# Taking the inverse sequence DFT of a spectral filter from radix 4 to radix 8, beside a gated MLP on the same core

## The chip, the cores and the metric

The kernel runs on one core of a Trainium2 chip. The metric is the device time of one execution in microseconds (us). The kernel before takes 262.6 us (median of 16 runs, 262.2 to 263.7). The record marks each execution as fast or slow by its time and its clock; every run that is quoted here is marked fast.

Engines are named as in the profile: PE (TensorE matmuls), PEld (its weight loads), DVE (VectorE), ACT (ScalarE), POOL (GpSimd), SP (the queue that issues most DMAs). "Start to start" is the distance between the starts of neighbouring instructions in the timeline. It is shorter than the duration of one record, because records of one engine overlap. PSUM is the memory in which the kernel keeps PE's results (tiles such as pd, gps, ups, dn, cs, ut, fp), SBUF the one for all other tiles. Line numbers such as L397 differ between kernels; the names of tiles do not.

## The reference, cut to what matters

```
xn = layernorm(x)                                  # x: 1 x 2048 x 512, bf16
A  = irfft2( rfft2(xn) * (w_r + 1j*w_i) )          # over sequence and features
B  = ( gelu(xn @ w_gate) * (xn @ w_up) ) @ w_down  # 512 -> 1792 -> 512
out = x + A + B
```

All the DFTs are done as matmuls with constant tables of cosines and sines. Along the sequence (2048) the DFT is split: the index is k = 2048/R·m + k0 and the position is s = R·t + r. A butterfly of radix R over m runs on DVE; a matmul over k0 runs on PE.

## The kernel before

Four groups of work matter.

- **MLP**: gps and ups (gate and up projection), then hT, then dn (down projection). It has 4 chunks of 14 column blocks. Per block PE runs 8 matmuls of 512 columns, ACT makes sq, gsb and sg, DVE makes wtl, z, m and hT. Each row block adds dn to x on DVE, into bsp.
- **Forward DFT**: pd (along features), then cs (along the sequence), then a radix-4 butterfly on DVE and the product with w_r + i·w_i (tiles qq, bf, XFk, tm).
- **Inverse along the sequence**: a radix-4 butterfly on DVE into YY, then the matmuls of ut with the table Rt, which ACT copies to UT.
- **Inverse along features**: fp, added to bsp on DVE, and out.

The instruction order of each engine is fixed when the kernel is built. Code marked `hp()` is placed as early as its inputs allow; everything else goes in program order, with the MLP ahead of the DFT's work on DVE.

The part that is changed, cut:

```python
for kc in range(4):                       # k = 512 m + 4 i + kc
    Fkc, WRk, WIk = ...                   # loaded by SP
    for r in range(4):
        cbsb = p3q.tile([P, 2, 256], BF16, tag="cbsb", bufs=2)
        ...  # cs: 2 x 4 matmuls of 512 columns, ACT copies to qq and cbsb, DVE adds
    ...  # radix-4 butterfly forward: 16 additions; product with w: 24
    ...  # radix-4 butterfly inverse: 16 additions into bi and YY, 4 negations, 8 tiny copies

UT = p3ut.tile([P, 4, 4, D], BF16)
Rt = p3r.tile([P, 4, 2, 4, D], BF16)      # 4 MB
nc.gpsimd.dma_start(out=Rt[:], in_=rview)
with hp():
  for rp in range(4):
    for t in range(4):
        ut = p3u.tile([P, D], FP32)
        for kc in range(4):
            for pi_, (lt, rh) in enumerate(pairs):   # two pairs: (YY part, Rt part)
                nc.tensor.matmul(ut[:], lhsT=lt, rhs=rh, ...)   # 512 columns
        nc.scalar.copy(out=UT[:, rp, t, :], in_=ut[:])
```

## Time and profile before

| | before |
|---|---|
| time, median | 262.6 us |
| span of the profiled run | 260.3 us |
| PE / DVE / ACT busy | 240.8 / 183.3 / 140.9 us |
| ut on PE | 187.5 to 215.4 us |
| last write to YY on DVE | 178.1 us |

The first part of the page of the kernel before, busy time, and its PE and DVE rows of 40 equal slices (each digit is the busy share in tenths):

```profile
PE 240.8 (92%) x1120; PEld 107.3 (41%) x1120; DVE 183.3 (70%) x613; ACT 140.9 (54%) x286; POOL 11.6 (4%) x20
PE   0398999999999999999999999999999999989993
DVE  3996844448996899997999999995820005872573
```

PE has work in nearly every slice after the first. DVE is nearly full from slice 10 to slice 27 (counted from 1) and idle in slices 31 to 33, under ut.

The table of stretches of the kernel before (stretch, its length, busy us and instructions of PE, PEld, DVE, ACT and POOL, granted clock, DMA share, GB/s):

```profile
10.00:60.00 50.00, 48.54 (x253) 23.48 (x254) 30.95 (x86) 40.54 (x83) 3.08 (x4) 1.00 0.52 170
60.00:180.00 120.00, 117.64 (x529) 50.81 (x528) 112.79 (x440) 69.60 (x150) 0.57 (x1) 1.00 0.19 64
180.00:248.00 68.00, 66.73 (x307) 29.79 (x306) 27.00 (x60) 28.85 (x52) 0.00 (x0) 1.00 0.10 43
```

From 60 to 180 us PE is idle for 2.4 us and DVE for 7.2 us.

The timeline of PE in the kernel before, around ut (start, length, engine, line, instruction, count):

```profile
186.87 0.81 PE L209 MATMUL ups<-xnT,wu 128*128 128x512 bf16 x3
187.51 28.04 PE L397 MATMUL ut<-Rt,YY 128*128 128x512 bf16 x128
215.39 0.38 PE L209 MATMUL ups<-xnT,wu 128*128 128x512 bf16 x1
```

ut is one unbroken block. From 187.51 to the next start at 215.39 are 27.88 us, 218 ns for each of 128 matmuls. The MLP is not finished then; it goes on afterwards.

The last instruction that writes YY, from the view of that tile (duration ns min/median/max, first and last start):

```profile
L365 DVE COPY YY<-YY x16: 143/152/156, 77.4 to 178.1; 128x1 bf16<-128x1 bf16 x16
```

PE's waits in the kernel before, the longest (who waited for whom, us in total, times, longest):

```profile
PE tp L189 <- DVE xn L183: 10.2, 2, 10.0
PE dn L234 <- DVE hT L229: 1.2, 2, 0.9
PE cs L295 <- ACT cbsb L291: 1.2, 3, 0.5
```

Ten of PE's 19.5 idle us are the start, before the first input has arrived and is normalised.

### The profile page before, as it was taken

Reading aid. Unit: us, or ns where it says so; the run is one execution under the profiler, and the core shown is the slowest. Engines: PE = TensorE matmul, PEld = TensorE weight load, DVE = VectorE, ACT = ScalarE, POOL = GpSimd, SP = SyncE. Lnnn points to the kernel's source line nnn. Section 1 sums busy time; section 2 is a strip of 40 time slices with the busy share of each in tenths; the row PEclk is TensorE's granted clock in tenths of the full one; section 3 lists DMA queues with packets and bytes.
Section 4 is the critical chain, followed back from the end, with each engine's and each line's share of the span. In section 5 each row is a group of like instructions: output and inputs, shape, how many; then the busy total and the mean of one; then the engine's idle time right before and its main releaser. Section 6 shows DMA issues by size and latency. Waiting matters only on the chain.

```text
span 260.3 us, 3447 instructions
## 1 busy us (share of the span) xinstructions
PE 240.8 (92%) x1120; PEld 107.3 (41%) x1120; DVE 183.3 (70%) x613; ACT 140.9 (54%) x286; POOL 11.6 (4%) x20
## 2 busy tenths in 40 slices
PE   0398999999999999999999999999999999989993
PEld 0354444444444444444444444344444444434441
DVE  3996844448996899997999999995820005872573
ACT  1489987768433587974155799422843336920000
POOL 8530000000000000000000000000000000000000
PEclk9999999999999999999999999999999999999999
DMA  7999930004041503000500000038500000000134
GB/s 251 356 337 371 323 99 1 0 3 161 0 109 36 181 0 81 4 1 20 181 21 23 0 0 0 20 95 382 233 3 0 0 0 1 3 1 0 43 120 161
DMA packets 10242, 23.56 MB, mean 91 GB/s; under 512 B 816, under 2 KB 7088, under 8 KB 9584
## 3 DMA queue, kind: packets, MB, share of 16 engines
q1 hardware_dynamic: 8400, 13.12, 15.2%
q0 software_dynamic: 1824, 10.22, 10.8%
q8 instruction: 9, 0.15, 0.2%
q14 instruction: 9, 0.07, 0.1%
HBM read 21.24 MB, written 2.10 MB: 90 GB/s over the span
## 4 chain that ended last, share of the span: by engine, by line
PE 45%; DVE 37%; ACT 11%; issue 4%; DMA 1%; DVEq 0%; ACTq 0%
PE ut L397 9%; DVE hT L229 7%; PE gps L203 7%; PE ups L209 7%; PE dn L234 6%; DVE z L224 5%; PE fp L415 5%; DVE m L228 4%; PE cs L295 4%; PE pd L264 3%; ACT sg L226 3%; PE cs L286 3%; ACT sq L215 2%; DVE bsp L241 2%; DVE stats L174 2%
## 5 line engine op out<-in xcount | busy, mean ns | idle before, releaser
L203 PE MATMUL gps<-xnT,wg 128*128 128x512 bf16 x224 | 60.9, 381 | 0.1
L209 PE MATMUL ups<-xnT,wu 128*128 128x512 bf16 x224 | 59.6, 379 | 0.1
L229 DVE TENSOR_TENSOR hT<-m,ups 128x512 bf16<-128x512 bf16 x56 | 38.3, 683 | 27.4 <-PE ups L209 25.2
L234 PE MATMUL dn<-wd,hT 128*128 128x512 bf16 x224 | 53.7, 379 | 1.7 <-DVE hT L229 1.2
L215 ACT ACTIVATE sq<-gps 128x512 bf16<-128x512 f32 x56 | 33.2, 593 | 20.6 <-PE gps L203 20.0
L226 ACT ACTIVATE sg<-z 128x512 bf16<-128x512 bf16 x56 | 35.3, 631 | 15.1 <-DVE z L224 13.4
L234 PEld LDWEIGHTS <-hT 128*128 128x128 bf16 x224 | 21.8, 97 | 30.9 <-DVE hT L229 3.7
L209 PEld LDWEIGHTS <-wu 128*128 128x128 bf16 x224 | 21.8, 98 | 27.1 <-issue 2.0
L217 ACT CAST gsb<-gps 128x512 bf16<-128x512 f32 x56 | 32.6, 582 | 0.0
L203 PEld LDWEIGHTS <-wg 128*128 128x128 bf16 x224 | 21.9, 98 | 25.2 <-issue 0.7
L228 DVE TENSOR_TENSOR m<-sg,gsb 128x512 bf16<-128x512 bf16 x56 | 23.6, 421 | 10.6 <-ACT sg L226 10.5
L397 PE MATMUL ut<-Rt,YY 128*128 128x512 bf16 x128 | 27.9, 379 | 0.1
L224 DVE TENSOR_TENSOR z<-wtl,gsb 128x512 bf16<-128x512 bf16 x56 | 23.6, 421 | 3.6 <-ACT gsb L217 2.8
L219 DVE TENSOR_SCALAR wtl<-sq 128x512 bf16<-128x512 bf16 x56 | 16.1, 288 | 8.1 <-ACT sq L215 8.1
L397 PEld LDWEIGHTS <-YY 128*128 128x128 bf16 x128 | 12.5, 98 | 15.3 <-issue 0.4
L286 PE MATMUL cs<-Pt,Fkc 128*128 128x512 bf16 x64 | 18.4, 379 | 0.2 <-ACT cbsb L300 0.2
L402 ACT CAST UT<-ut 128x512 bf16<-128x512 f32 x16 | 9.3, 584 | 16.2 <-PE ut L397 16.2
L241 DVE TENSOR_TENSOR bsp<-xblk,dn 128x512 bf16<-128x512 bf16 x16 | 10.9, 683 | 9.8 <-PE dn L234 9.8
L295 PE MATMUL cs<-Pt,Fkc 128*128 128x512 bf16 x64 | 16.4, 378 | 1.3 <-ACT cbsb L291 1.2
L189 PE MATMUL tp<-ident,xn 128*128 128x128 bf16 x64 | 7.1, 254 | 11.2 <-DVE xn L183 10.2
L264 PE MATMUL pd<-Gt,xnT 128*128 128x512 bf16 x64 | 16.4, 379 | 0.0
L415 PE MATMUL fp<-Ginv,UT 128*128 128x512 bf16 x64 | 15.2, 378 | 0.3 <-DVE osb L419 0.3
(65 smaller groups left out, 200.0 us busy)
## 6 DMA issues: line engine op xcount, KB each, us to landing
Fkc<-cF SPq DMA_DIRECT2D x4, 1024.0 KB, 4.9
Rt<-cR POOLq DMA_DIRECT2D x1, 4096.0 KB, 12.7
xt<-in_A_x_dram SPq DMA_DIRECT2D x4, 512.0 KB, 5.8
xblk<-in_A_x_dram SPq DMA_DIRECT2D x16, 128.0 KB, 3.0
out_dram<-osb SPq DMA_DIRECT2D x4, 512.0 KB, 2.6
wd<-in_B_w_down_dram POOLq DMA_DIRECT2D x2, 896.0 KB, 16.2
wg<-in_B_w_gate_dram POOLq DMA_DIRECT2D x4, 384.0 KB, 16.0
wu<-in_B_w_up_dram POOLq DMA_DIRECT2D x4, 384.0 KB, 16.0
```

The lines of the kernel that those rows point to most:

```text
L203: nc.tensor.matmul(gps[:], lhsT=wg[:, dt, fc * P:(fc + 1) * P], rhs=xnT[:, dt, 4 * c:4 * c + 4, :], start=(dt == 0), stop=(dt == 3),)
L209: nc.tensor.matmul(ups[:], lhsT=wu[:, dt, fc * P:(fc + 1) * P], rhs=xnT[:, dt, 4 * c:4 * c + 4, :], start=(dt == 0), stop=(dt == 3),)
L215: nc.scalar.activation(out=sq[:], in_=gps[:], func=ACT.Square)
L217: nc.scalar.copy(out=gsb[:], in_=gps[:])
L224: tt(out=z[:], in0=wtl[:], in1=gsb[:], op=ALU.mult)
L226: nc.scalar.activation(out=sg[:], in_=z[:], func=ACT.Sigmoid, scale=2.0)
L228: tt(out=m1[:], in0=sg[:], in1=gsb[:], op=ALU.mult)
L229: tt(out=hT[:, fc, :], in0=m1[:], in1=ups[:], op=ALU.mult)
L234: nc.tensor.matmul(dn[:], lhsT=hT[:, fc, r * P:(r + 1) * P], rhs=wd[:, fc, :], start=(fc == 0), stop=(fc == 13),)
L295: nc.tensor.matmul(cs2[:], lhsT=Fkc[:, 1, b, :], rhs=Pt[:, b, :], start=(T == 0), stop=(T == 3),)
L397: nc.tensor.matmul(ut[:], lhsT=lt, rhs=rh, start=(kc == 0 and pi_ == 0), stop=(kc == 3 and pi_ == 1),)
L415: nc.tensor.matmul(fp[:], lhsT=UT[:, r, t, c * P:(c + 1) * P], rhs=Ginv[:, t, :], start=(t == 0), stop=(t == 3),)
```

## The change

The butterfly after the product takes 8 values instead of 4. What remains for the matmul is a sum over 256 instead of 512 frequencies, so each of the 8 values of r has an output only 256 columns wide. The number of ut matmuls stays at 128 (8 r, 4 tiles, 2 halves q, 2 parts); their width halves. The table Rt halves to 2 MB. On DVE, two radix-8 butterflies replace four radix-4 ones: 52 additions and 4 scalings each, against 16 additions each. To fit in memory, cbsb, WRk, WIk and tm lose their second buffers; XFk gets a second one, because two blocks now feed one butterfly. x is viewed as rows 8·tau + rho, so the forward tables and the loads of x are permuted too. The forward DFT stays at radix 4.

The core of the diff:

```diff
-        for kc in range(4):
+        for kc in (0, 2, 1, 3):
...
-                cbsb = p3q.tile([P, 2, 256], BF16, tag="cbsb", bufs=2)
+                cbsb = p3q.tile([P, 2, 256], BF16, tag="cbsb", bufs=1)
...
-            tt(out=bi[:, 0, 0, 0:257], in0=z0r, in1=z2r, op=ALU.add)
-            ... (16 additions, 4 negations, 8 tiny copies for each kc)
+            if kc >= 2:
+                q = kc - 2
+                ... ins: 8 values, even ones from XF_by_kc[q], odd ones from XF_by_kc[kc]
+                dft8(ins, outs_, SC)        # 52 additions, 4 scalings
+                ... (8 negations, 16 tiny copies)
...
-        Rt = p3r.tile([P, 4, 2, 4, D], BF16)
+    Rt = p3r.tile([P, 2, 2, 8, 256], BF16)
...
-        for rp in range(4):
+            for rp in range(8):
                 for t in range(4):
-                ut = p3u.tile([P, D], FP32)
-                for kc in range(4):
+                    if t % 2 == 0:
+                        ut2 = p3u.tile([P, 2, 256], FP32)
+                    ut = ut2[:, t % 2, :]
+                    for q in range(2):
...
-                nc.scalar.copy(out=UT[:, rp, t, :], in_=ut[:])
+                    if t % 2 == 1:
+                        nc.scalar.copy(out=UT[:, rp, t - 1:t + 1, :], in_=ut2[:])
```

dft8 itself, cut:

```python
comb4([ins[0], ins[2], ins[4], ins[6]], A)      # 16 additions
comb4([ins[1], ins[3], ins[5], ins[7]], B)      # 16 additions
# t1 = B[1] * e^(i pi/4), t3 = B[3] * e^(3 i pi/4): 4 additions, 4 scalings
# outs = A +- (B[0], t1, i B[2], t3): 16 additions
```

More of the change, by code (lines that the diff above doesn't have):

```diff
@@ L52, in _host_constants @@
     tau = np.arange(P).astype(np.int64)
-    T = np.arange(4).astype(np.int64)
-    rho = np.arange(4).astype(np.int64)
-    iv = np.arange(P).astype(np.int64)
-    qv = np.arange(4).astype(np.int64)
-    s_val = (512 * T[:, None, None] + 4 * tau[None, :, None] + rho[None, None, :])
+    T8 = np.arange(2).astype(np.int64)
+    rho8 = np.arange(8).astype(np.int64)
+    mp = np.arange(P).astype(np.int64)
+    kcv = np.arange(4).astype(np.int64)
+    s_val = (1024 * T8[:, None, None] + 8 * tau[None, :, None] + rho8[None, None, :])
     sv = s_val.transpose(1, 0, 2)
-    prod = (4 * iv[None, None, None, None, :] + qv[:, None, None, None, None]) * sv[None, :, :, :, None]
+    prod = (128 * kcv[:, None, None, None, None] + mp[None, None, None, None, :]) * sv[None, :, :, :, None]
     angF = 2.0 * np.pi * (prod % S) / S
@@ L63, in _host_constants @@
     F = np.stack([Fcos, Fsin], axis=2).reshape(4, P, 2 * 16 * P)
-    tp = np.arange(D).astype(np.int64)
-    rv = np.arange(4).astype(np.int64)
-    kp = 4 * iv[:, None] + qv[None, :]
-    sp = 4 * tp[None, :] + rv[:, None]
+    ii = np.arange(P).astype(np.int64)
+    qv = np.arange(2).astype(np.int64)
+    tp = np.arange(256).astype(np.int64)
+    rv = np.arange(8).astype(np.int64)
+    kp = 128 * qv[None, :] + ii[:, None]
+    sp = 8 * tp[None, :] + rv[:, None]
     angR = 2.0 * np.pi * ((kp[:, :, None, None] * sp[None, None, :, :]) % S) / S
     R = np.stack([np.cos(angR), np.sin(angR)], axis=2)
-    R = R.reshape(P, 4 * 2 * 4 * D)
+    R = R.reshape(P, 2 * 2 * 8 * 256)
     bf = ml_dtypes.bfloat16
@@ L101 @@
     x2 = A_x[0]
-    xv = x2.rearrange("(T tau rho) d -> tau T rho d", T=4, tau=P, rho=4)
-    ov = out[0].rearrange("(T tau rho) d -> T tau rho d", T=4, tau=P, rho=4)
+    xv = x2.rearrange("(T tau rho) d -> tau T rho d", T=2, tau=P, rho=8)
+    ov = out[0].rearrange("(T tau rho) d -> T tau rho d", T=2, tau=P, rho=8)
     wgv = B_w_gate.rearrange("(p dt) f -> p dt f", dt=4)
@@ L108 @@
     giview = cGinv.rearrange("(kt p) d -> p kt d", p=P)
-    rview = cR.rearrange("i (kc cs r t) -> i kc cs r t", kc=4, cs=2, r=4)
+    rview = cR.rearrange("i (q cs r t) -> i q cs r t", q=2, cs=2, r=8)
+    wrv4 = A_w_r.rearrange("(m kc i) k -> i kc m k", m=4, kc=4)
+    wiv4 = A_w_i.rearrange("(m kc i) k -> i kc m k", m=4, kc=4)
     tt = nc.vector.tensor_tensor
@@ L113, with cadd, csub, dft8 @@
     hp = lambda: tc.high_priority(offset=HP_OFF)
+    def cadd(o, a, b_):
+        tt(out=o, in0=a, in1=b_, op=ALU.add)
+    def csub(o, a, b_):
+        tt(out=o, in0=a, in1=b_, op=ALU.subtract)
+    def dft8(ins, outs, sc):
+        def cx(slot):
+            return (sc[:, slot, 0, 0:257], sc[:, slot, 1, 0:257])
+        def comb4(e, A):
+            (s02r, s02i), (d02r, d02i), (s13r, s13i), (d13r, d13i) = cx(0), cx(1), cx(2), cx(3)
+            cadd(s02r, e[0][0], e[2][0])
+            cadd(s02i, e[0][1], e[2][1])
+            csub(d02r, e[0][0], e[2][0])
+            csub(d02i, e[0][1], e[2][1])
+            cadd(s13r, e[1][0], e[3][0])
+            cadd(s13i, e[1][1], e[3][1])
+            csub(d13r, e[1][0], e[3][0])
+            csub(d13i, e[1][1], e[3][1])
+            cadd(A[0][0], s02r, s13r)
+            cadd(A[0][1], s02i, s13i)
+            csub(A[2][0], s02r, s13r)
+            csub(A[2][1], s02i, s13i)
+            csub(A[1][0], d02r, d13i)
+            cadd(A[1][1], d02i, d13r)
+            cadd(A[3][0], d02r, d13i)
+            csub(A[3][1], d02i, d13r)
+        A = [outs[0], outs[1], outs[2], outs[3]]
+        comb4([ins[0], ins[2], ins[4], ins[6]], A)
+        B = [cx(4), cx(5), cx(6), cx(7)]
+        comb4([ins[1], ins[3], ins[5], ins[7]], B)
+        cinv = float(1.0 / np.sqrt(2.0))
+        t1r, t1i = cx(0)
+        t3r, t3i = cx(1)
+        csub(t1r, B[1][0], B[1][1])
+        cadd(t1i, B[1][0], B[1][1])
+        nc.vector.tensor_scalar(out=t1r, in0=t1r, scalar1=cinv, scalar2=None, op0=ALU.mult)
+        nc.vector.tensor_scalar(out=t1i, in0=t1i, scalar1=cinv, scalar2=None, op0=ALU.mult)
+        cadd(t3r, B[3][0], B[3][1])
+        csub(t3i, B[3][0], B[3][1])
+        nc.vector.tensor_scalar(out=t3r, in0=t3r, scalar1=-cinv, scalar2=None, op0=ALU.mult)
+        nc.vector.tensor_scalar(out=t3i, in0=t3i, scalar1=cinv, scalar2=None, op0=ALU.mult)
+        csub(outs[4][0], A[0][0], B[0][0])
+        csub(outs[4][1], A[0][1], B[0][1])
+        cadd(outs[0][0], A[0][0], B[0][0])
+        cadd(outs[0][1], A[0][1], B[0][1])
+        csub(outs[5][0], A[1][0], t1r)
+        csub(outs[5][1], A[1][1], t1i)
+        cadd(outs[1][0], A[1][0], t1r)
+        cadd(outs[1][1], A[1][1], t1i)
+        cadd(outs[6][0], A[2][0], B[2][1])
+        csub(outs[6][1], A[2][1], B[2][0])
+        csub(outs[2][0], A[2][0], B[2][1])
+        cadd(outs[2][1], A[2][1], B[2][0])
+        csub(outs[7][0], A[3][0], t3r)
+        csub(outs[7][1], A[3][1], t3i)
+        cadd(outs[3][0], A[3][0], t3r)
+        cadd(outs[3][1], A[3][1], t3i)
@@ L135 @@
     ) as p1ps:
-        xt = p1.tile([P, 4, 4, D], BF16)
+        xt = p1.tile([P, 2, 8, D], BF16)
         wpieces = [(0, 2), (2, 5), (5, 8), (8, 11), (11, 14)]
@@ L145, in wu_dma @@
             nc.gpsimd.dma_start(out=wu[:, :, a * P:b_ * P], in_=wuv[:, :, a * P:b_ * P])
-        nc.sync.dma_start(out=xt[:, 0, :, :], in_=xv[:, 0, :, :])
+        xq = [(0, 0), (0, 4), (1, 0), (1, 4)]
+        nc.sync.dma_start(out=xt[:, 0, 0:4, :], in_=xv[:, 0, 0:4, :])
         wg_dma(0)
@@ L151 @@
         wu_dma(1)
-        nc.sync.dma_start(out=xt[:, 1, :, :], in_=xv[:, 1, :, :])
+        nc.sync.dma_start(out=xt[:, 0, 4:8, :], in_=xv[:, 0, 4:8, :])
         nc.gpsimd.dma_start(out=wd[:, 0:7, :], in_=wdv[:, 0:7, :])
@@ L155 @@
         wu_dma(2)
-        nc.sync.dma_start(out=xt[:, 2, :, :], in_=xv[:, 2, :, :])
+        nc.sync.dma_start(out=xt[:, 1, 0:4, :], in_=xv[:, 1, 0:4, :])
         nc.gpsimd.dma_start(out=wd[:, 7:14, :], in_=wdv[:, 7:14, :])
@@ L159 @@
         wu_dma(3)
-        nc.sync.dma_start(out=xt[:, 3, :, :], in_=xv[:, 3, :, :])
+        nc.sync.dma_start(out=xt[:, 1, 4:8, :], in_=xv[:, 1, 4:8, :])
         wg_dma(4)
@@ L169 @@
         rstd = p1.tile([P, 16], FP32)
-        xn = p1.tile([P, 4, 4, D], BF16)
-        for T in range(4):
-            for r in range(4):
-                b = 4 * T + r
+        xn = p1.tile([P, 2, 8, D], BF16)
+        for hb in range(4):
+            T, r0 = xq[hb]
+            b0 = 8 * T + r0
+            for r in range(r0, r0 + 4):
+                b = 8 * T + r
                 nc.vector.bn_stats(out=stats[:, b, :], in_=xt[:, T, r, :])
@@ L176 @@
             nc.scalar.activation(
-                out=sd[:, 4 * T:4 * T + 4], in_=mv[:, 4 * T:4 * T + 4, 1],
+                out=sd[:, b0:b0 + 4], in_=mv[:, b0:b0 + 4, 1],
                 func=ACT.Sqrt, bias=epsb[:], scale=1.0,
             )
-            nc.vector.reciprocal(out=rstd[:, 4 * T:4 * T + 4], in_=sd[:, 4 * T:4 * T + 4])
-            for r in range(4):
-                b = 4 * T + r
+            nc.vector.reciprocal(out=rstd[:, b0:b0 + 4], in_=sd[:, b0:b0 + 4])
+            for r in range(r0, r0 + 4):
+                b = 8 * T + r
                 nc.vector.tensor_scalar(
@@ L231 @@
             b = 4 * c + r
+            Tb, rr = b // 8, b % 8
             dn = psA.tile([P, D], FP32, bufs=1)
@@ L238 @@
             xblk = mpool.tile([P, D], BF16, tag="xblk", bufs=4)
-            nc.sync.dma_start(out=xblk[:], in_=xv[:, c, r, :])
+            nc.sync.dma_start(out=xblk[:], in_=xv[:, Tb, rr, :])
             bsp = mpool.tile([P, D], BF16, tag="bsp", bufs=16)
@@ L242 @@
             bsp_tiles[b] = bsp
-    wrv4 = A_w_r.rearrange("(m i q) k -> i q m k", m=4, q=4)
-    wiv4 = A_w_i.rearrange("(m i q) k -> i q m k", m=4, q=4)
     p3yy = ctx.enter_context(tc.tile_pool(name="p3yy", bufs=1))
-    YY = p3yy.tile([P, 4, 4, 3, 258], BF16)
-    bi = p3yy.tile([P, 2, 4, 258], BF16)
+    YY = p3yy.tile([P, 2, 8, 3, 258], BF16)
+    SC = p3yy.tile([P, 8, 2, 258], BF16)
     with tc.tile_pool(name="p3f", bufs=1) as p3f, tc.tile_pool(
@@ L253 @@
         name="p3q", bufs=1
-    ) as p3q, tc.tile_pool(name="p3xf", bufs=1) as p3xf, tc.tile_pool(
-        name="p3w", bufs=2
+    ) as p3q, tc.tile_pool(name="p3xf", bufs=2) as p3xf, tc.tile_pool(
+        name="p3w", bufs=1
     ) as p3w, tc.tile_pool(name="p3cs", bufs=1, space=bass.MemoryType.PSUM) as p3cs:
         Pt = p3f.tile([P, 16, D], BF16)
+        blocks4 = [[8 * T8 + r4 + 4 * hi for T8 in range(2) for hi in range(2)]
+                   for r4 in range(4)]
         with hp():
-            for r in range(4):
-                for T in range(4):
-                    b = 4 * T + r
+            for r4 in range(4):
+                for b in blocks4[r4]:
                     pd = p3ps.tile([P, D], FP32)
@@ L268 @@
                     nc.scalar.copy(out=Pt[:, b, :], in_=pd[:])
-        for kc in range(4):
+        XF_by_kc = {}
+        for kc in (0, 2, 1, 3):
             Fkc = p3g.tile([P, 2, 16, P], BF16)
@@ L280 @@
             for r in range(4):
-                cbsb = p3q.tile([P, 2, 256], BF16, tag="cbsb", bufs=2)
+                cbsb = p3q.tile([P, 2, 256], BF16, tag="cbsb", bufs=1)
                 with hp():
                     cs = p3cs.tile([P, D], FP32, tag="cs")
-                    for T in range(4):
-                        b = 4 * T + r
+                    for n, b in enumerate(blocks4[r]):
                         nc.tensor.matmul(
                             cs[:], lhsT=Fkc[:, 0, b, :], rhs=Pt[:, b, :],
-                            start=(T == 0), stop=(T == 3),
+                            start=(n == 0), stop=(n == 3),
                         )
@@ L292 @@
                     cs2 = p3cs.tile([P, D], FP32, tag="cs")
-                    for T in range(4):
-                        b = 4 * T + r
+                    for n, b in enumerate(blocks4[r]):
                         nc.tensor.matmul(
                             cs2[:], lhsT=Fkc[:, 1, b, :], rhs=Pt[:, b, :],
-                            start=(T == 0), stop=(T == 3),
+                            start=(n == 0), stop=(n == 3),
                         )
@@ L313 @@
             XFk = p3xf.tile([P, 4, 2, 258], BF16)
+            XF_by_kc[kc] = XFk
             tt(out=XFk[:, 0, 0, 0:257], in0=s02r, in1=s13r, op=ALU.add)
@@ L333 @@
                 tt(out=XFk[:, m, 1, 0:257], in0=tm[:, 2, 0:257], in1=tm[:, 3, 0:257], op=ALU.subtract)
-            z0r, z1r, z2r, z3r = (XFk[:, m, 0, 0:257] for m in range(4))
-            z0i, z1i, z2i, z3i = (XFk[:, m, 1, 0:257] for m in range(4))
-            tt(out=bi[:, 0, 0, 0:257], in0=z0r, in1=z2r, op=ALU.add)
-            tt(out=bi[:, 0, 1, 0:257], in0=z0r, in1=z2r, op=ALU.subtract)
-            tt(out=bi[:, 0, 2, 0:257], in0=z1r, in1=z3r, op=ALU.add)
-            tt(out=bi[:, 0, 3, 0:257], in0=z1r, in1=z3r, op=ALU.subtract)
@@ L340 @@
-            tt(out=bi[:, 1, 0, 0:257], in0=z0i, in1=z2i, op=ALU.add)
-            tt(out=bi[:, 1, 1, 0:257], in0=z0i, in1=z2i, op=ALU.subtract)
-            tt(out=bi[:, 1, 2, 0:257], in0=z1i, in1=z3i, op=ALU.add)
-            tt(out=bi[:, 1, 3, 0:257], in0=z1i, in1=z3i, op=ALU.subtract)
-            s02r, d02r, s13r, d13r = (bi[:, 0, k, 0:257] for k in range(4))
-            s02i, d02i, s13i, d13i = (bi[:, 1, k, 0:257] for k in range(4))
-            outs_ = {
-                0: [(s02r, s13r, ALU.add), (s02i, s13i, ALU.add)],
-                2: [(s02r, s13r, ALU.subtract), (s02i, s13i, ALU.subtract)],
-                1: [(d02r, d13i, ALU.subtract), (d02i, d13r, ALU.add)],
-                3: [(d02r, d13i, ALU.add), (d02i, d13r, ALU.subtract)],
-            }
@@ L352 @@
-            for rp in range(4):
-                (a0, a1, opr), (b0, b1, opi) = outs_[rp]
-                R_ = YY[:, kc, rp, 0, 0:257]
-                I_ = YY[:, kc, rp, 1, 0:257]
-                N_ = YY[:, kc, rp, 2, 0:257]
-                tt(out=R_, in0=a0, in1=a1, op=opr)
-                tt(out=I_, in0=b0, in1=b1, op=opi)
-                nc.vector.tensor_scalar(
-                    out=N_, in0=I_, scalar1=-1.0, scalar2=None, op0=ALU.mult
-                )
-                nc.vector.tensor_copy(
-                    out=YY[:, kc, rp, 1, 256:257], in_=YY[:, kc, rp, 0, 256:257]
-                )
-                nc.vector.tensor_copy(
-                    out=YY[:, kc, rp, 0, 256:257], in_=YY[:, kc, rp, 2, 256:257]
-                )
+            if kc >= 2:
+                q = kc - 2
+                Xe, Xo = XF_by_kc[q], XF_by_kc[kc]
+                ins = []
+                for m8 in range(8):
+                    src = Xe if m8 % 2 == 0 else Xo
+                    m4 = m8 // 2
+                    ins.append((src[:, m4, 0, 0:257], src[:, m4, 1, 0:257]))
+                outs_ = [(YY[:, q, rp, 0, 0:257], YY[:, q, rp, 1, 0:257]) for rp in range(8)]
+                dft8(ins, outs_, SC)
+                for rp in range(8):
+                    nc.vector.tensor_scalar(
+                        out=YY[:, q, rp, 2, 0:257], in0=YY[:, q, rp, 1, 0:257],
+                        scalar1=-1.0, scalar2=None, op0=ALU.mult,
+                    )
+                    nc.vector.tensor_copy(
+                        out=YY[:, q, rp, 1, 256:257], in_=YY[:, q, rp, 0, 256:257]
+                    )
+                    nc.vector.tensor_copy(
+                        out=YY[:, q, rp, 0, 256:257], in_=YY[:, q, rp, 2, 256:257]
+                    )
@@ L369 @@
+    p3r = ctx.enter_context(tc.tile_pool(name="p3r", bufs=1))
+    Rt = p3r.tile([P, 2, 2, 8, 256], BF16)
     p3ut = ctx.enter_context(tc.tile_pool(name="p3ut", bufs=1))
-    UT = p3ut.tile([P, 4, 4, D], BF16)
-    with tc.tile_pool(name="p3r", bufs=1) as p3r, tc.tile_pool(
+    UT = p3ut.tile([P, 8, 4, 256], BF16)
+    with tc.tile_pool(
         name="p3u", bufs=2, space=bass.MemoryType.PSUM
     ) as p3u:
-        Rt = p3r.tile([P, 4, 2, 4, D], BF16)
         nc.gpsimd.dma_start(out=Rt[:], in_=rview)
-        hpi = hp()
-        hpi.__enter__()
-        for rp in range(4):
-            for t in range(4):
-                ut = p3u.tile([P, D], FP32)
-                for kc in range(4):
-                    Rcs = Rt[:, kc, 0, rp, :]
-                    Rsn = Rt[:, kc, 1, rp, :]
-                    if t == 0:
-                        pairs = [(YY[:, kc, rp, 0, 0:128], Rcs),
-                                 (YY[:, kc, rp, 2, 0:128], Rsn)]
-                    elif t == 1:
-                        pairs = [(YY[:, kc, rp, 0, 128:256], Rcs),
-                                 (YY[:, kc, rp, 2, 128:256], Rsn)]
-                    elif t == 2:
-                        pairs = [(YY[:, kc, rp, 0, 1:129], Rsn),
-                                 (YY[:, kc, rp, 1, 1:129], Rcs)]
-                    else:
-                        pairs = [(YY[:, kc, rp, 0, 129:257], Rsn),
-                                 (YY[:, kc, rp, 1, 129:257], Rcs)]
-                    for pi_, (lt, rh) in enumerate(pairs):
-                        nc.tensor.matmul(
-                            ut[:], lhsT=lt, rhs=rh,
-                            start=(kc == 0 and pi_ == 0),
-                            stop=(kc == 3 and pi_ == 1),
-                        )
-                nc.scalar.copy(out=UT[:, rp, t, :], in_=ut[:])
-        hpi.__exit__(None, None, None)
@@ new lines @@
+        with hp():
+            for rp in range(8):
+                for t in range(4):
+                    if t % 2 == 0:
+                        ut2 = p3u.tile([P, 2, 256], FP32)
+                    ut = ut2[:, t % 2, :]
+                    for q in range(2):
+                        Rcs = Rt[:, q, 0, rp, :]
+                        Rsn = Rt[:, q, 1, rp, :]
+                        if t == 0:
+                            pairs = [(YY[:, q, rp, 0, 0:128], Rcs),
+                                     (YY[:, q, rp, 2, 0:128], Rsn)]
+                        elif t == 1:
+                            pairs = [(YY[:, q, rp, 0, 128:256], Rcs),
+                                     (YY[:, q, rp, 2, 128:256], Rsn)]
+                        elif t == 2:
+                            pairs = [(YY[:, q, rp, 0, 1:129], Rsn),
+                                     (YY[:, q, rp, 1, 1:129], Rcs)]
+                        else:
+                            pairs = [(YY[:, q, rp, 0, 129:257], Rsn),
+                                     (YY[:, q, rp, 1, 129:257], Rcs)]
+                        for pi_, (lt, rh) in enumerate(pairs):
+                            nc.tensor.matmul(
+                                ut, lhsT=lt, rhs=rh,
+                                start=(q == 0 and pi_ == 0),
+                                stop=(q == 1 and pi_ == 1),
+                            )
+                    if t % 2 == 1:
+                        nc.scalar.copy(out=UT[:, rp, t - 1:t + 1, :], in_=ut2[:])
@@ L407 @@
     ) as p4ps:
-        for c in range(4):
-            osb = p4.tile([P, 4, D], BF16)
-            for r in range(4):
-                b = 4 * c + r
+        for aT in range(2):
+            osb = p4.tile([P, 8, D], BF16)
+            for rp in range(8):
+                b = 8 * aT + rp
                 bb = bsp_tiles[b]
@@ L415 @@
                     nc.tensor.matmul(
-                        fp[:], lhsT=UT[:, r, t, c * P:(c + 1) * P], rhs=Ginv[:, t, :],
+                        fp[:], lhsT=UT[:, rp, t, aT * P:(aT + 1) * P], rhs=Ginv[:, t, :],
                         start=(t == 0), stop=(t == 3),
                     )
-                tt(out=osb[:, r, :], in0=bb[:], in1=fp[:], op=ALU.add)
-            nc.sync.dma_start(out=ov[c], in_=osb[:])
+                tt(out=osb[:, rp, :], in0=bb[:], in1=fp[:], op=ALU.add)
+                if rp % 4 == 3:
+                    nc.sync.dma_start(out=ov[aT][:, rp - 3:rp + 1, :], in_=osb[:, rp - 3:rp + 1, :])
 _INS = ['A_x', 'A_w_r', 'A_w_i', 'B_x', 'B_w_gate', 'B_w_up', 'B_w_down']
```

## The prediction

> **What bounds it now.** TensorE. The page gives PE 240.8 us of a 260.3 us span (92%), DVE 70%, ACT 54%; the table of stretches has PE at 9.1 to 10 us of every 10 from 10 to 250 us. PE has few holes, about 2.4 us between 60 and 180 us; the granted clock is full. DVE is the near second: 7 us idle between 60 and 180 us.
>
> **What is removed.** The row-direction inverse DFT (tile ut) goes from radix 4 to radix 8: still 128 matmuls, each 256 columns wide instead of 512. In the timeline ut is one unbroken block on PE, 187.5 to 215.5 us: 27.9/128 = 218 ns a matmul, weight loads hidden. The Trainium skill ("TensorE: Matmul & The Clock Gate", Back-to-back issue gap) has the gap as columns/2.4 + 2.5 ns: 216 ns at 512, which this trace bears out, and 109 at 256, which it does not show; 128-column transposes do run at about 70 ns here, loads included. I estimate 112 ns, 14.3 us for ut, so **13.6 us less PE work** (240.8 to about 227). The Rt transfer halves (4 MB to 2 MB) and no longer has to wait for the last tm products; today it is issued at 173.9 and lands at 186.6, 8.5 us after the last YY write at 178.
>
> **What is added.** Two radix-8 butterflies replace four radix-4 ones: 104 additions against 64, plus 8 scalings. A 257-wide addition takes 0.203 us start to start in the timeline (bi, 134.6 to 136.3), a scaling about 0.14: +8.1 +1.1 = **+9.2 us of DVE**. It is low-priority work that fills DVE's gaps in the MLP; PE has MLP matmuls to run meanwhile. But YY comes later: an MLP column block costs PE 2.6 us (with its share of dn) and DVE 1.65 us, so DVE has about 36% to spare while PE does MLP, and 9.2 us more needs about 25 us: last YY write near 203 instead of 178. PE's filler (MLP, cs, pd; 240.8 - 28 - 14 = 199 us from 10 us on) lasts until about 210. So it should just fit, with ut moved from 187 to about 200-208, behind most of the MLP. If YY is late, DVE is freed of MLP work and catches up: the loss is bounded. The single buffers for cbsb, WR, WI and tm shorten the lead of the cs chain and can add PE waits; cs already waits 1.4 us for cbsb. The end (fp, last output) is the same.
>
> **Sum.** 262.9 - 13.6 = 249.3; I add 2.5 us for new PE waits (YY late, cbsb): **252 us, range 247 to 259**. Faster by over 2%: 0.84, within 2%: 0.14, slower: 0.02.
>
> **What would show the steps right or wrong.**
> - ut busy about 14 us, 128 matmuls at about 112 ns start to start (groups, timeline). If near 150 ns or more, weight loads are no longer hidden.
> - DVE busy about 192 us.
> - First ut matmul at 197-210 us, with little or no idle before it released by DVE YY; Rt long landed.
> - PE busy near 227 us, its holes near 20 us as before (mostly the first 10 us and the end).
>
> **What would make it wrong.** PE idle before ut because DVE is the bound (then the gain shrinks by that hole, perhaps 5 us or more); weight loads limiting 256-column matmuls; the static instruction order being bad for the longer DVE chain, so PE waits on hT or cs; the serial load of WR/WI, now behind the last tm of the block before, holding back XF and YY.

## The result, and the profile after

The changed kernel takes **250.9 us** (median of 10 runs, 249.7 to 252.2). One more execution, 252.9 us and also fast, is not among the ten; with it the median would be 251.0. The ratio to the kernel before is 0.9545, 95% interval 0.9523 to 0.9566. Here and below a ratio is the one for the fast runs of the same rounds; it is not quite the ratio of the medians quoted.

| | before | after |
|---|---|---|
| time, median | 262.6 us | 250.9 us |
| span of the profiled run | 260.3 us | 247.7 us |
| PE busy | 240.8 us | 227.6 us |
| DVE busy | 183.3 us | 191.0 us |
| main block of ut starts | 187.5 us | 199.1 us |
| last write to YY | 178.1 us | 201.0 us |

Busy time and the PE and DVE rows of the kernel after:

```profile
PE 227.6 (92%) x1120; PEld 107.2 (43%) x1120; DVE 191.0 (77%) x661; ACT 140.4 (57%) x286; POOL 11.5 (5%) x20
PE   0298999999999999999999999999999999999992
DVE  2998664345999999999946999999999960462473
```

PE's busy time fell by 13.2 us and its share stayed at 92%: the span shrank with it. DVE is now nearly full from slice 11 to slice 32, with a gap in slices 21 and 22: the longer butterflies spread into the time that it had free after YY.

The same stretches of the kernel after:

```profile
60.00:180.00 120.00, 117.88 (x532) 51.31 (x531) 113.35 (x438) 70.19 (x151) 0.55 (x1) 1.00 0.22 70
180.00:248.00 68.00, 61.96 (x342) 32.89 (x340) 40.70 (x121) 28.39 (x52) 0.00 (x0) 1.00 0.09 33
```

From 60 to 180 us nothing changed for PE. The additional DVE work sits after 180 us (40.7 us instead of 27.0). The kernel before has another 6.7 us of DVE work after 248 us, when the changed one has ended, so to the end of each it is 40.7 against 33.7 us: 7.0 of the 7.7 us that DVE's busy time grew.

The timeline of PE in the kernel after, around the main block of ut:

```profile
195.38 0.72 PE L454 MATMUL ut<-Rt,YY 128*128 128x256 bf16 x5 [0.36 <-DVE YY L413]
...
199.13 11.61 PE L454 MATMUL ut<-Rt,YY 128*128 128x256 bf16 x104
210.57 1.03 PE L271 MATMUL gps<-xnT,wg 128*128 128x512 bf16 x4
```

The 104 matmuls from 199.13 to 210.57 us take 110.0 ns each. The holes before ut that DVE ends are short, such as the 0.36 us in brackets.

The last write to YY, and PE's waits, in the kernel after:

```profile
L420 DVE COPY YY<-YY x16: 146/149/156, 120.3 to 201.0; 128x1 bf16<-128x1 bf16 x16
```

```profile
PE tp L257 <- DVE xn L251: 10.8, 1, 10.8
PE cs L362 <- ACT cbsb L359: 0.5, 2, 0.3
PE ut L454 <- DVE YY L413: 0.4, 1, 0.4
PE ut L454 <- DVE YY L120: 0.3, 1, 0.3
```

The YY tile is finished 23 us later than before, and PE waits 0.7 us for it in all. When the last write lands, ut is already running on the earlier values of r.

### The profile page after: what moved, and what is told of

Read it like the earlier page. It is cut to its first block, busy times and chain, and to the rows that moved or that the text cites. A ratio compares the mean times of both kernels' runs of the same rounds, so it can differ in the third digit from the quotient of the medians.

```text
span 247.7 us, 3491 instructions
## 1 busy us (share of the span) xinstructions
PE 227.6 (92%) x1120; PEld 107.2 (43%) x1120; DVE 191.0 (77%) x661; ACT 140.4 (57%) x286; POOL 11.5 (5%) x20
## 4 chain that ended last, share of the span: by engine, by line
PE 47%; DVE 38%; ACT 9%; issue 3%; DMA 2%; DVEq 0%; ACTq 0%
PE ups L277 9%; PE gps L271 8%; DVE hT L297 7%; PE dn L303 6%; PE ut L454 6%; PE fp L472 5%; DVE z L292 5%; PE cs L362 4%; DVE m L296 4%; PE pd L332 4%; PE cs L354 3%; DVE bsp L310 3%; ACT sg L294 3%; DVE stats L242 2%; DVE wtl L287 2%
## 5 line engine op out<-in xcount | busy, mean ns | idle before, releaser
L277 PE MATMUL ups<-xnT,wu 128*128 128x512 bf16 x224 | 60.9, 379 | 0.3 <-DVE hT L297 0.2
L354 PE MATMUL cs<-Pt,Fkc 128*128 128x512 bf16 x64 | 18.4, 378 | 0.2 <-ACT cbsb L367 0.2
L454 PE MATMUL ut<-Rt,YY 128*128 128x256 bf16 x128 | 15.2, 273 | 0.6 <-DVE YY L413 0.4
L242 DVE BATCH_NORM_STATS2 stats<-xt 128x6 f32<-128x512 bf16 x16 | 10.4, 663 | 4.1 <-DMA xt<-in_A_x_dram 4.1
```

The lines of the kernel that those rows point to most:

```text
L277: nc.tensor.matmul(ups[:], lhsT=wu[:, dt, fc * P:(fc + 1) * P], rhs=xnT[:, dt, 4 * c:4 * c + 4, :], start=(dt == 0), stop=(dt == 3),)
L454: nc.tensor.matmul(ut, lhsT=lt, rhs=rh, start=(q == 0 and pi_ == 0), stop=(q == 1 and pi_ == 1),)
```

## The experiments

The theory: the gain is the PE time of the half-width matmuls, all of it on the critical path, and the added DVE work is hidden behind MLP work that PE still has. The rivals: the gain comes from the smaller, earlier Rt transfer or from the new order; or DVE is already a second bound and eats part of the gain. Each experiment was timed in 3 rounds beside the kernel before, which took 262.6 to 263.0 us each time.

| run | time, median | ratio to before (95%) | last YY write |
|---|---|---|---|
| before | 262.6 | 1 | 178.1 |
| after | 250.9 | 0.9545 (0.9523 to 0.9566) | 201.0 |
| ut_twice | 266.3 | 1.0129 (1.0110 to 1.0148) | 200.6 |
| before_half | 250.1 | 0.9507 (0.9481 to 0.9533) | 179.6 |
| dft_cheap | 250.4 | 0.9525 (0.9507 to 0.9543) | 160.2 |
| dft_plus1 | 255.4 | 0.9712 (0.9684 to 0.9741) | 219.1 |
| dft_plus2 | 263.7 | 1.0015 (0.9990 to 1.0040) | 228.8 |
| cbsb2 | 250.9 | 0.9547 (0.9514 to 0.9580) | 186.7 |
| after_h | 251.1 | 0.9547 (0.9525 to 0.9568) | 185.5 |
| fwd8 | 252.2 | 0.9590 (0.9550 to 0.9630) | 218.1 |
| fwd8_h | 242.5 | 0.9223 (0.9180 to 0.9267) | 209.3 |
| fwd8_g | 243.4 | 0.9253 (0.9226 to 0.9280) | 209.5 |
| fwd8_f | 244.0 | 0.9257 (0.9201 to 0.9313) | 202.8 |
| fwd8_fg | 239.6 | 0.9113 (0.9080 to 0.9146) | 203.4 |

### Is it the PE time? ut_twice and before_half

ut_twice, on the changed kernel:

```diff
+                    for pas in range(2):
-                    for q in range(2):
+                        for q in range(2):
                             ... (the four matmuls of this ut, start and stop as they were)
```

> The changed kernel with each group of four half-width ut matmuls run twice; the second pass starts the sum anew, so the result stays right. Theory (the gain is the PE time of half-width matmuls, all of it on the critical path): 128 more matmuls at the 110 ns start to start that the trace of after shows are 14.1 us, so about 265 us (262.5 to 266.5), as slow as the kernel before or slower. Rival (the gain came from the halved and earlier Rt transfer, or from the new order of instructions): those stay, so it stays below 257 us.

Measured: 266.3 us, correct. Giving PE the same 128 half-width matmuls once more costs 15.4 us. 14.1 us of that are the matmuls; a wait of 1.5 us at cs for the Fkc transfer, which its profile has and that of after has not, is about the rest. The whole gain is gone although Rt is small, early and loaded in the new way. The Rt rival falls.

before_half, on the kernel before (its result is wrong, because half of each ut is computed and used twice):

```diff
-                            ut[:], lhsT=lt, rhs=rh,
+                            ut[:, 0:256], lhsT=lt, rhs=rh[:, 0:256],
...
-                nc.scalar.copy(out=UT[:, rp, t, :], in_=ut[:])
+                nc.scalar.copy(out=UT[:, rp, t, :].rearrange("p (h c) -> p h c", h=2),
+                               in_=ut[:, 0:256].unsqueeze(1).to_broadcast([P, 2, 256]))
```

> The kernel before with only the width of its ut matmuls halved to 256 columns, the eviction reading the 256 columns twice (wrong result on purpose); DVE work, buffers and the 4 MB Rt load as before. Theory: 13.8 us less on PE, all of it gained: 247.5 to 250 us, that is 1 to 3 us faster than after, and that difference is what the rest of the change costs. Rival (the half width alone is worth little, because Rt lands at 186 us or DVE holds the end): 254 us or more.

Measured: 250.1 us, just above the range expected. The width alone gives 12.7 us. All the rest of the change (radix-8 butterflies, single buffers, the new view of x) costs 0.0038 of 262.7, about 1.0 us; the two intervals overlap, so this is uncertain by some 0.9 us (an estimate from their widths). Some 0.7 us is found at the very start. The DVE timeline of the kernel before and then of the kernel after, first statistics of x:

```profile
4.16 1.28 DVE L174 BATCH_NORM_STATS2 stats<-xt 128x6 f32<-128x512 bf16 x2 [3.29 <-DMA xt<-in_A_x_dram]
```

```profile
4.98 1.29 DVE L242 BATCH_NORM_STATS2 stats<-xt 128x6 f32<-128x512 bf16 x2 [4.11 <-DMA xt<-in_A_x_dram]
```

DVE waits 3.29 us for the first piece of x before and 4.11 us after. In the two traces with the old view of x this wait is 3.2 and 3.3 us, in the twelve with the new view 3.8 to 4.1 us. The new view reads half of each 8 KB group of rows at first where the old one read whole 4 KB groups. That this is the reason was not tested.

### How much DVE work is hidden? dft_cheap, dft_plus1, dft_plus2

dft_cheap takes the added DVE work away from the changed kernel (wrong result):

```diff
         comb4([ins[0], ins[2], ins[4], ins[6]], A)
-        B = [cx(4), cx(5), cx(6), cx(7)]
-        ... (the other half, t1 and t3, the 16 last additions)
+        comb4([ins[1], ins[3], ins[5], ins[7]], outs[4:8])
```

> The changed kernel with the radix-8 butterfly cut to two radix-4 ones (32 additions each, no scaling; wrong result on purpose): the 9.2 us of DVE work that the change added is gone. Theory (added DVE work is hidden behind the PE's remaining MLP work): 249.5 to 251.5 us, within 1.5 us of after, though the last YY write moves from about 201 to about 180 us. Rival (DVE is already a second bound and costs part of the gain): 248 us or less.

Measured: 250.4 us, no different from after. Its last write to YY came at 160 us, 41 us earlier than in after, earlier even than forecast, and it bought nothing. So in after the added work is hidden in full.

dft_plus1 and dft_plus2 repeat 20 additions and 4 scalings of each butterfly once and twice (the repeats are idempotent, the results correct):

```diff
-        comb4([ins[1], ins[3], ins[5], ins[7]], B)
+        for _ in range(2):                         # 3 in dft_plus2
+            comb4([ins[1], ins[3], ins[5], ins[7]], B)
...
+        for _ in range(2):                         # 3 in dft_plus2
             ... (t1 and t3: 4 additions, 4 scalings)
```

> The changed kernel with 20 additions and 4 scalings of each radix-8 butterfly done twice (idempotent, right result): another 9.2 us of DVE work. Theory: PE still has about 17 us of MLP work left (3 column pairs and the last dn blocks) when ut starts at 199 us in after, so most of the delay is still filled: 251 to 254 us, last YY write at 212 to 218 us and a first hole on PE before ut. Rival (no slack left, DVE on the chain in full): about 260 us. Rival (DVE never matters): 250.9 us and no hole.

> As dft_plus1 with the part done three times: 18.4 us of DVE work over after. dft_plus1 cost 4.5 us, so about half of its 9.2 us was still hidden; no slack should be left now, and the next 9.2 us should show in full: 262 to 266 us (rival, slack still there or self-correcting: 260 us or less). The holes on PE should be at dn (waiting for bsp and hT) and at ut (waiting for YY), 15 us or more between them.

Measured: 255.4 and 263.7 us. From dft_cheap to after, 9.2 us of DVE work cost 0.5 us, inside the noise. The next 9.2 us cost 4.5, the next 8.3. So the change used up slack that was there, and left some of it, about 5 us if 9.2 - 4.5 is taken as an estimate. The 4.5 and 8.3 us are not the price of DVE's time alone. In the profile of dft_plus1 PE also waits 1.9 us for Fkc, as it did 1.5 us in ut_twice, which has no added DVE work. And the clock fell: the mean granted clock was 0.999 in the profiled run of dft_plus1 (254.4 us, the fastest), 0.992 in its three others, and 0.986 or 0.987 in all five of dft_plus2. dft_plus1 was 1.4 us over its range, its last write to YY 1.1 us after the range forecast, and the hole was not where it was expected. PE's timeline of dft_plus1:

```profile
207.53 0.39 PE L305 MATMUL dn<-wd,hT 128*128 128x512 bf16 x1 [1.42 <-DVE hT L299]
208.73 3.18 PE L305 MATMUL dn<-wd,hT 128*128 128x512 bf16 x14 [0.81 <-DVE bsp L312]
212.99 1.02 PE L305 MATMUL dn<-wd,hT 128*128 128x512 bf16 x4 [1.08 <-DVE bsp L312]
```

PE did not run out of MLP work and then wait for YY. Its last MLP work was itself held up: dn has one PSUM buffer, which the addition into bsp on DVE frees, and that addition stood in DVE's fixed order among the butterflies. Filler work that needs the crowded engine is not free filler. In dft_plus2 waits of 3.7 and 2.1 us for YY come on top; with 4.3 us for bsp and 1.1 us for hT they make 11.2 us, less than the 15 us forecast. Its last 112 ut matmuls then take 14.06 us, where those of dft_plus1 take 12.39: the granted clock was 0.50 from 226 to 232 us.

### Do the single buffers hold the gain back? cbsb2

```diff
-                cbsb = p3q.tile([P, 2, 256], BF16, tag="cbsb", bufs=1)
+                cbsb = p3q.tile([P, 2, 256], BF16, tag="cbsb", bufs=2)
```

The first form of this run gave WRk, WIk and tm their second buffers too; it did not fit in memory and never ran. What those would do is open.

> The changed kernel with cbsb in two buffers again, as before (WR, WI and tm can't have theirs back: their pool then no longer fits in memory). In after PE waits 0.7 us in all for ACT's cbsb copies. Theory (the single buffers cost next to nothing): 250 to 251.5 us. Rival (the shorter lead of the cs chain is what holds back a part of the gain): 249.5 us or less.

Measured: 250.9 us, as after. But the last write to YY moved from 201.0 to 186.7 us. The view of YY in dft_cheap, then in cbsb2:

```profile
L392 DVE COPY YY<-YY x16: 138/148/157, 83.3 to 160.2; 128x1 bf16<-128x1 bf16 x16
L420 DVE COPY YY<-YY x16: 136/147/157, 119.0 to 186.7; 128x1 bf16<-128x1 bf16 x16
```

So two things bear on the date: from after, a second cbsb buffer (and the order of instructions that goes with it) takes away 14 us, and taking out the added DVE work takes away 41 us (dft_cheap, still with the single buffer). Each of the two edits also shifts the fixed order of instructions. They do not add up to the 23 us by which after is later than before, so that delay cannot be divided between the two. As PE had other work, none of these dates mattered.

### Taking it further: fwd8, and relief for DVE

If PE is the bound, the forward sequence DFT (cs) can be halved in the same way. fwd8 does so. It uses the first two of the four forward tables and dft8 again:

```diff
-        for kc in (0, 2, 1, 3):
+        for q in range(2):
...
-            for r in range(4):
+            for r in range(8):
...
-                    for n, b in enumerate(blocks4[r]):
+                    for n, b in enumerate((r, 8 + r)):
...
-            ... (radix-4 butterfly through bf)
+            dft8(ins, xf, SC)
```

To fit, tm lives in SC and xblk has three buffers instead of four.

> The changed kernel with the forward column DFT (tile cs) taken to radix 8 too: 64 cs matmuls of 512 columns instead of 128, 13.9 us less PE; forward butterflies of radix 8 for radix 4, 9.2 us more DVE, as much as dft_plus1 added. If PE alone were the bound: 250.9 - 13.9 = 237 us. Theory of two bounds (PE and the DVE chain to the last YY): dft_plus1 showed that 9.2 us more DVE work already costs 4.5 us with the PE's work unchanged; with less PE work to hide under, more of it shows: 241 to 248 us, PE waiting 10 us or more in the last third for DVE.

Measured: 252.2 us, correct. PE has 64 matmuls of 512 columns less to do (64 × 217 ns = 13.9 us), and the kernel became no faster than after. It missed its range upwards. The run to compare it with for PE's part is dft_plus1, which has as much added DVE work: against its 255.4 us, fwd8 gained 3.2 us. PE's timeline of fwd8:

```profile
194.52 0.39 PE L303 MATMUL dn<-wd,hT 128*128 128x512 bf16 x1 [1.42 <-DVE hT L297]
195.73 4.87 PE L303 MATMUL dn<-wd,hT 128*128 128x512 bf16 x14 [0.81 <-DVE bsp L310]
201.37 3.18 PE L303 MATMUL dn<-wd,hT 128*128 128x512 bf16 x14 [0.78 <-DVE bsp L310]
205.63 3.18 PE L303 MATMUL dn<-wd,hT 128*128 128x512 bf16 x14 [1.08 <-DVE bsp L310]
213.49 1.25 PE L428 MATMUL ut<-Rt,YY 128*128 128x256 bf16 x5 [4.68 <-DVE YY L120]
216.27 1.68 PE L428 MATMUL ut<-Rt,YY 128*128 128x256 bf16 x7 [1.53 <-DVE YY L387]
218.19 13.09 PE L428 MATMUL ut<-Rt,YY 128*128 128x256 bf16 x112 [0.25 <-ACT UT L434]
```

This is DVE's chain, with holes of 10.3 us on PE in the brackets of the first six lines. Two groups are also slow in themselves: 14 dn matmuls take 4.87 us, where their neighbours take 3.18, and 112 ut matmuls take 13.09 us where dft_plus1 and fwd8_g need 12.39. The table of stretches of fwd8 shows the granted clock (the number after POOL's):

```profile
193.00:195.00 2.00, 0.49 (x2) 0.11 (x2) 2.00 (x9) 0.18 (x1) 0.00 (x0) 1.00 0.00 0
197.00:199.00 2.00, 2.00 (x6) 0.69 (x5) 2.00 (x11) 0.00 (x0) 0.00 (x0) 0.50 0.13 37
213.00:216.00 3.00, 1.25 (x5) 0.57 (x5) 3.00 (x17) 0.00 (x0) 0.00 (x0) 0.50 0.00 0
```

After the holes the clock was halved for a while, so idle time on PE cost more than itself. The two slow groups add 1.7 and 0.7 us. The slow dn group also held DVE up in turn: by the timeline of DVE, the bsp addition at 200.63 us waited 1.29 us for dn, in the middle of the work that leads to YY.

Now DVE was to be relieved. Its costliest single group is hT, which reads ups from PSUM: it takes 0.60 us start to start, against 0.34 us for z, of the same size, with both inputs in SBUF. The Trainium skill ("VectorE: DVE Perf Modes", section "The perf-mode tier table (the rule you actually need)") lists `tensor_tensor` at 2x for bf16 in SBUF and 1x with any operand in PSUM; this trace agrees in kind. fwd8_h lets ACT, 54% busy, do the copy for every second block; fwd8_f does it for all:

```diff
-            tt(out=hT[:, fc, :], in0=m1[:], in1=ups[:], op=ALU.mult)
+            if fc % 2 == 1:              # fwd8_f: True
+                nc.scalar.copy(out=hT[:, fc, :], in_=ups[:])
+                tt(out=hT[:, fc, :], in0=m1[:], in1=hT[:, fc, :], op=ALU.mult)
+            else:
+                tt(out=hT[:, fc, :], in0=m1[:], in1=ups[:], op=ALU.mult)
```

> fwd8 with DVE relieved: for every second MLP column block ACT copies ups out of PSUM into hT as bf16, and DVE multiplies there (about 0.34 us in place of 0.60 us, from z and hT in the trace), 28 times: 7.3 us less DVE, 16 us more ACT (54% busy). Theory of two bounds: 3 to 7 us faster than fwd8. Rival (PE or its order of instructions is the bound in fwd8): within 1 us of fwd8.

> fwd8 with ACT copying ups out for all 56 column blocks: 14.6 us less DVE, 33 us more ACT (about 173 us of 240). Theory of two bounds: as fast as fwd8_h or up to 3 us faster, unless ACT's queue becomes the new wait (then slower than fwd8_h, with PE waiting for gps buffers that ACT has not freed).

Measured: 242.5 us for fwd8_h, 9.8 us faster than fwd8 and more than forecast; 244.0 us for fwd8_f, whose interval overlaps that of fwd8_h. ACT's busy time grew by 10.6 and 24.1 us, less than the 16 and 33 us forecast. Both profiles have the clock below full for some microseconds in the last quarter, and PE waits for hT (2.7 us in fwd8_h, 4.0 us in fwd8_f).

after_h is the control: the same relief as fwd8_h, on the changed kernel, without the halved cs.

> Control for fwd8_h: the changed kernel, forward DFT left at radix 4, with ups copied out by ACT for every second column block (7.3 us less DVE). Theory: in after PE alone is the bound (dft_cheap, with less DVE work, was no faster), so 249 to 251.5 us, and the 8 us that fwd8_h gained need both parts. Rival (the ACT copy itself is what helped fwd8_h, by freeing PSUM or relieving DVE): 246 us or less.

Measured: 251.1 us, as after, though DVE was relieved and the last write to YY came at 185.5 us. Relief for DVE is worth nothing where PE is the bound (after_h), 13.9 us less PE work bought with 9.2 us more DVE work is worth nothing (fwd8), and the two together gain about 8 us over after (fwd8_h).

fwd8_g and fwd8_fg give dn two PSUM buffers and ups two instead of three, on fwd8_h and fwd8_f:

```diff
-            ups = psA.tile([P, D], FP32, bufs=3)
+            ups = psA.tile([P, D], FP32, bufs=2)
...
-            dn = psA.tile([P, D], FP32, bufs=1)
+            dn = psA.tile([P, D], FP32, bufs=2)
```

> fwd8_h with dn in two PSUM buffers instead of one and ups in two instead of three. In fwd8_h PE waits 2.9 us for DVE's bsp additions, which free the single dn buffer, about 2.4 of them at 196 to 206 us, and around 195 us the granted clock falls to 0.50 for 3 us. Theory: those waits go: 239 to 242 us, 0 to 3 us faster than fwd8_h. Rival (the time is set by the last YY write on DVE, at 209 us): same as fwd8_h within 1 us; and if ups needs its third buffer, slower.

> fwd8_f (ups copied out by ACT for all 56 column blocks) with dn in two PSUM buffers and ups in two. In fwd8_g the dn waits went, and ut then waited for the last YY write at 209 us; in fwd8_f that write is at 202 us, but PE waited 4 us for hT and dn and its clock fell. Theory (the end is the last YY write, then ut 12.4 us, fp 14.6 us and the output 4 us, as long as PE has no holes before): 235 to 240 us, faster than fwd8_h. Rival (ACT at 163 us, holding gps buffers, is now the bound): 242 us or more.

Measured: 243.4 us for fwd8_g, no gain over fwd8_h: the rival was right. The waits at dn went, and PE waited for YY in their place. PE's timeline of fwd8_g:

```profile
207.63 0.94 PE L432 MATMUL ut<-Rt,YY 128*128 128x256 bf16 x7 [2.00 <-DVE YY L391]
```

fwd8_fg takes **239.6 us** (239.2 to 239.8, correct). It is 8.9% faster than the kernel before, and by the medians 4.5% faster than the change. Its busy times and the end of its PE timeline:

```profile
PE 214.9 (90%) x1037; PEld 101.3 (43%) x1056; DVE 185.7 (78%) x709; ACT 160.5 (67%) x342; POOL 11.5 (5%) x20
```

```profile
201.55 0.94 PE L432 MATMUL ut<-Rt,YY 128*128 128x256 bf16 x7
202.32 0.38 PE L307 MATMUL dn<-wd,hT 128*128 128x512 bf16 x1
202.94 12.39 PE L432 MATMUL ut<-Rt,YY 128*128 128x256 bf16 x112 [0.24 <-ACT UT L438]
215.38 3.83 PE L307 MATMUL dn<-wd,hT 128*128 128x512 bf16 x17
```

YY is ready at 203.4 us while PE still has dn work, some of it left over until after ut, and the mean granted clock is 1.0. (19 of its matmul records are missing in the trace.) The second dn buffer only paid once DVE's chain was short enough: with half the relief it turned one wait into another.

## Why the prediction was right or wrong, point by point

**The time: right.** Forecast 252 us, range 247 to 259; measured 250.9 us.

**PE is the bound: right, and shown** by ut_twice (PE time put back, gain gone), before_half (PE time alone, gain there) and dft_cheap (DVE time taken away, nothing gained).

**The size of the PE saving: right.** Forecast 112 ns a matmul and 13.6 us; measured 110.0 ns and 13.2 us less PE busy time. The formula of the Trainium skill ("TensorE: Matmul & The Clock Gate", "Back-to-back issue gap": columns/2.4 + 2.5 ns), which the page calls the gap of a single matmul in isolation, comes to 109 ns for 256 columns; this trace now shows it to hold with a weight load before each matmul. The loads stay hidden at 256 columns.

**DVE busy about 192 us: right**, 191.0 us.

**YY ready near 203 us: right in number, not in reason.** It came at 201.0 us. The prediction derived the delay of 25 us from 9.2 us of DVE work at 36% of spare DVE time. The runs follow no such rate: 9.2 us of DVE work moved the last write by 41 us (dft_cheap to after), then by 18 (to dft_plus1), then by 10 (to dft_plus2), and cbsb2, with the DVE work of after, was ready at 186.7 us, 8.6 us later than before. That the sum agreed was luck.

**"First ut matmul at 197-210 us": right for the block, not for the first.** 104 of the 128 ran in one block from 199.1 us; the other 24 ran in small groups among the MLP from 169.7 us on, a mixture that the prediction did not have.

**"It should just fit": right.** It fitted with some room: 9.2 us more of DVE work cost 4.5 us, and 18.4 cost 12.8 (263.7 - 250.9).

**"If YY is late, DVE is freed of MLP work and catches up: the loss is bounded": wrong.** From dft_plus1 to dft_plus2, 9.2 us more DVE work cost 8.3 us. Past the slack there was little catching up: DVE had no MLP work left to be freed of but the bsp additions (from 207.5 us on, its timeline in dft_plus2 has only those and the butterfly work that leads to YY). In dft_plus2 and fwd8 the lower clock even added to the loss.

**The 2.5 us for new PE waits: too much, and in the wrong place.** The whole rest of the change costs about 1.0 us (after against before_half). Waits for YY and cbsb are not it: PE waits 0.7 us for YY and 0.7 us for cbsb in after, and cbsb2 was no faster. About 0.7 us is the later arrival of the first piece of x, a term that the prediction did not have. Why before_half gains 12.7 us where its matmuls shrink by 13.8 us (128 × 108 ns) is open to about 1 us; 0.43 us of it is a wait of PE for ACT's copy to UT in its profile.

**"The serial load of WR/WI holding back XF and YY"** was named as a danger and could not be tested on its own, for want of memory.

## What to carry to other kernels

When a change moves work from the engine that is the bound to another, find out how much room the other has up to the date at which its result is needed, not over the whole span: here DVE was 70% busy, yet the trade was free for the first 9 us, about half price for the next 9, and nearly full price after that, the lower clock included. To see which engine sets the time, give it back its work or take the other's away, one at a time; an early result (YY at 160 us) or a shorter queue shows nothing until the time moves. And when the second bound is reached, the next step must take from both: halving cs alone (with the DVE work that it adds) gained nothing, relieving DVE alone gained nothing, and the two, with one PSUM buffer moved from ups to dn, gained 4.5% over the change.

## What the Trainium skill lacked or had wrong

- "TensorE: Matmul & The Clock Gate", section "Back-to-back issue gap", says that a real kernel's stream of weight loads and matmuls sustains about 131 ns a matmul at 512 columns and that columns/2.4 + 2.5 ns overcounts there. Here it does not: 218 ns at 512 columns (ut before, 128 in a row) and 110.0 ns at 256 (ut after, 104 in a row), each matmul with its own weight load. The simple formula (216 and 109 ns) was right.
- The same page, section "Why this matters for your kernels", advises no idle gaps of PE over about 3 us. In fwd8 two holes of 1.42 and 0.81 us with a single matmul between them were followed by a granted clock of 0.50 for about 3 us. A pair of holes of the same lengths in the profiled run of dft_plus1 left it at 1.00 (its three other runs, at a mean clock of 0.992, have no trace here). So keeping to that advice was not enough in fwd8. The page does say elsewhere that frequent short idles between groups of matmuls can lower the clock, but gives no lengths; what decides was not tested.
- "Perfetto Trace Analysis", section "Identifying the Most-Contended Engine", prefers MFU (the share of the peak arithmetic rate) and the weight loads' busy share to the busy share of matmuls as signs of how near PE is to its limit. MFU was not worked out here. Here weight loads were busy 41% before and 43% after, while PE was the bound (ut_twice: 14.1 us more of matmuls cost 15.4 us). With 512-column matmuls that share says little; matmul busy (92%) and the holes between matmuls told the truth.
- "VectorE: DVE Perf Modes", section "Rules for kernel authors", advises copying a matmul's output out of PSUM first only if many operations will use it. In this case a copy for a single use paid, because ACT made it and DVE was the bound: with it and a second dn buffer the forward radix-8 kernel went from 252.2 to 239.6 us.
- No page that I looked up has a number for what a changed view of the input costs at the start: the first 512 KB of x was waited for 3.2 to 3.3 us in the old view and 3.8 to 4.1 us in the new one.
